# Two more chunks through seven block products, and weighted sums over 32 keys for two query blocks

## Chip, cores and metric

The kernel runs on one core of one Trainium2 chip. The metric is the device time of one execution in microseconds (us), the median of several runs. Times in the profile come from one further execution that the hardware profiler recorded. All arithmetic is fp32; matmuls run on pieces of fp32 numbers (below).

## The reference

```python
def _attn_ref(q, k, v):                       # B, H, S, D = 8, 8, 576, 64
    scores = np.matmul(q, k.transpose(0, 1, 3, 2)) / np.sqrt(D)
    rel = pos[:, None] - pos[None, :]
    mask_local = (rel >= 0) & (rel < 32)                        # heads 0 to 3
    mask_strided = (rel >= 0) & (pos[None] % 32 == pos[:, None] % 32)   # 4 to 7
    ...                                       # masked softmax over the keys
    return np.matmul(attn, v)

def _moe_ref(x, w_in, w_out):                 # x 4608x512, w_in 512x2048
    h = x @ w_in
    g = np.maximum(h, 0.0) + np.log1p(np.exp(-np.abs(h)))       # softplus
    return g @ w_out                          # w_out 2048x512

x = attn_out.transpose(0, 2, 1, 3).reshape(B * S, H * D)
return _moe_ref(x, w_in, w_out)
```

So: sparse attention, then a layer of 2048 softplus units for each of 4608 tokens, then a second layer back to 512.

## The kernel before

**Feed-forward part.** The 4608 tokens are cut into nine *chunks* of 512 (NCHUNK = 9, numbered from 0). The hidden layer of a chunk has NFC = 16 *rows* f of 128 units (HALF = 8 of them are half the layer). The 512 features are four blocks of 128. Each fp32 operand of a matmul is split into a high and a low part (x_h and x_l, gh and gl), and each block is three matmuls: high by high, high by the weights' low part, low by high. `hidden(c, f)` (line 774) makes hidden row f of chunk c in a PSUM buffer ph: four blocks by three, 12 matmuls of 128x512. Softplus of it is three steps on ScalarE (lines 786, 789, 791) and one on VectorE (line 798); ScalarE or VectorE rounds it to gh (line 290), VectorE takes the difference gl (line 828). `output(c, f)` (line 843) adds row f to the chunk's four result banks py0 to py3 (one for each 128 tokens t): 12 matmuls again. After its last row a copy on ScalarE or VectorE (`result`, line 290) brings each bank out of PSUM.

**Seven block products.** For two neighbouring chunks A and A+1, and rows f and f+HALF, the first layer is a two by two product of blocks (chunks by rows, over halves of the features). `pair_of_chunks(A, ...)` makes it in Strassen's way with seven products of six matmuls (`product`, line 946, banks a, b and c) in place of eight: 42 matmuls for 48. One such round is a *lap*; between its products stand output matmuls. Around it come evictions of banks on ScalarE (`keep`, line 1037), joining additions on VectorE (`join`, line 1042), sums of blocks of x (`x_whole`, `x_sum`, `x_sum_low`: lines 972, 978, 988; `x_sum_high` rounds on ScalarE), and sums of blocks of the weights, which are made once (`w_task`: lines 994, 1007, 1017), stored to DRAM and loaded again for each lap (`w_sum_load`, `w_near_load`, `w_away_load`). Chunks 5 and 6 go through 7 laps, 7 and 8 through 8 laps. Of chunk 6 the softplus rows are stored to DRAM and loaded again when its outputs come (`u_store`, `u_load`; it is in SPILLED); the rows of 5 and 6 that no lap makes (PLAIN: 7 and 15) are made by `hidden` beforehand.

**Attention part.** Two heads at a time make a *pair*; there are 32 pairs n, four for each batch element. Pairs 0 to 7 belong to the start, whose order is a text list, FIRST. From pair 8 on the path is: loads of q, k and v; `head_scores` (line 422, called S*n* in the plan), which multiplies 64 queries by 32 keys at a time into PSUM tiles ps and po, using a quarter of TensorE's array for each; the mask added (line 481), the softmax; `turn` on VectorE, which transposes the probabilities in three steps (a whole tile, line 550, and two halves again, lines 555 and 557); `late_sums` (line 574, V*n* in the plan), the weighted sums of v: 36 matmuls over 64 keys for 32 queries each into PSUM; and `x_part`, which casts the result to x_h (line 691, on ScalarE) and subtracts for x_l (line 689, on VectorE). x_far is a tile of x beside x_h. The sums of pair n mostly stand in one *joint* event with the scores of pair n+1, back to back on TensorE; a pair in `alone` has them by itself. Both borrow the PSUM buffers ph and the banks, so a hidden row behind them waits until `x_part` has read them out.

**What sets the order.** Each engine runs its instructions in the order in which the program issues them. From row 2 of chunk 1 on a planner sets it (class `Plan`): every piece is a task with an engine, a cost, a time at which it is due, and the tasks it comes after (S and V as above, F hidden row, O output, y result, P `turn`, L `x_part`, X and W sums of x and of weights, j joining, k eviction, Us and Ul stored and loaded rows). The list `steps` (chunk, row) is the order of hidden rows; `pair_at` says behind which of them a pair's scores stand: before, pairs 8 to 27 behind every third row, and pairs 28 to 31 inside laps 0, 2, 4 and 6 of chunks 5 and 6 (`events`). Loads and stores are issued by SyncE (SP). NEAR is the first chunk that goes through block products: `NEAR = NCHUNK - 4`.

Of the kernel before, what the change touches and what calls it, by code (L numbers as in the profile page):

```python
# [18 lines left out]
P = 128  # L19
# [97 lines left out]
def attention_softplus_ffn(  # L117
# [94 lines left out]
    turned = homes[1][:, 2 * S : 3 * S].rearrange("p (c x l) -> p c x l", c=2, l=32)  # L212
# [31 lines left out]
    ROWS[-4] = sum(both[-1:] + both[:-1], [])  # L244
    ROWS[-3] = ROWS[-4]
# [31 lines left out]
    raws = {}  # L277

# [35 lines left out]
    def load_v(n):  # L314
        b, pair = order[n]
        if n >= 2 * NPAIR:
            if n == 2 * NPAIR:
# [12 lines left out]
            return  # L330
# [71 lines left out]
    def place_of(part, h):  # L402

        return 1 - h if part == 1 else h

    def head_scores(n):
# [5 lines left out]
        for x in range(6):  # L412
            for chunk in (x, x + 3) if x > 2 else (x,):
                part = chunk // 6
                for place in range(2):
                    a, i = block_at(chunk, place) if n < 2 * NPAIR else (3 * place, chunk)
                    c = TILE * a + 32 * i
                    for h in range(2):
                        to = 64 * place + 32 * place_of(part, h)
# [126 lines left out]
    def turn(n, step):  # L546

        src = prob_of(n).rearrange("p x (c l) -> p c x l", l=32)
        if step == 0:
            nc.vector.transpose(turned, src)  # L550
            return
        for place in range(2):
            lower, upper = (slice(at, at + 32) for at in (64 * place, 64 * place + 32))
            if step == 1:
                nc.vector.transpose(turned[upper, 0], src[lower, 1])
            else:
                nc.vector.transpose(turned[lower, 1], src[upper, 0])

    def late_sums(n, joint):
# [9 lines left out]
        pos[n, 0], pos[n, 1] = to  # L569
        for x in range(NCHK):  # L570
# [290 lines left out]
    sums_r, sums_c, banks = {}, {}, {}  # L861
# [94 lines left out]
    def stage(A, i, w):  # L956

        k = {"a": 0, "b": 1, "c": 2}[w] + 3 * i
        if A < NCHUNK - 2:
            if i == 0:  # L960
                return half_of(("xw", A, k // 2), f"wi{8+k//2}", k % 2)
            if (A, w) not in sums_r:
                sums_r[A, w] = io_pool.tile([P, DM], F32, tag="io", name=f"xw_{w}_{A}")
            return sums_r[A, w]
# [25 lines left out]
    def w_whole(r, f):  # L990

        t = sums_c[r, f] = io_pool.tile([P, DM], F32, tag="io", name=f"ww_{r}_{f}")
        w = w_i(4, f + r * HALF).bitcast(F32)
# [33 lines left out]
    def w_near_load(A, f):  # L1027
        nc.sync.dma_start(w_near(A).bitcast(F32), far_w[f])

# [175 lines left out]
    for i in range(begin, len(steps)):  # L1205
# [28 lines left out]
        for t in range(nt):  # L1234
# [23 lines left out]
    def scores_of(n, x, y, name, e, cost, after, also=None):  # L1258
# [28 lines left out]
        for j, (name, step, cost) in enumerate(  # L1287
            ((f"P{n}.0", 0, 0.8), (f"P{n}.1", 1, 0.95), (f"P{n}", 2, 0.95))
        ):
            fn = lambda step=step: turn(n, step)  # L1290
            add(name, y + 8.5 + 0.9 * j, "DVE", cost, fn, after)
# [8 lines left out]
    def parts_of(n, z, made):  # L1300
# [3 lines left out]
        for c in range(NCHUNK):  # L1304
            if START[c] < first + S and START[c] + CH[c] > first:
                old = [k for k in range(c) if PLACE[k] == PLACE[c]]
                if old:
# [14 lines left out]
    for i, n in pair_at.items():  # L1322
# [5 lines left out]
        scores_of(n, x, x + 1.5, f"S{n}", "PE", cost, after, n - 1 if joint(i) else None)  # L1328
        if n == far_first:
            made, z = f"V{n}", when[i + 3] + 0.6  # L1330
            add(made, when[i + 3], "PE", 1.3, lambda n=n: sums_of(n), [f"P{n}", f"v{n}"])
        else:
            made, z = f"S{n+1}", when[i_of[n + 1]] + 1.9
        parts_of(n, z, made)
# [14 lines left out]
    def out_task(c, f, t, late=()):  # L1349
# [16 lines left out]
        e, cost, engine = (("ACT", 0.6, nc.scalar), ("DVE", 0.7, nc.vector))[t % 2 * (c > NEAR)]  # L1366
# [3 lines left out]
    u_users = [f"Us{len(steps) - 2}", f"l{len(steps) - 1}"]  # L1370
# [10 lines left out]
    def g_task(c, f, z, src, after):  # L1381
# [4 lines left out]
        e, cost, engine = ("ACT", 0.65, nc.scalar) if c in SPILLED else ("DVE", 0.45, nc.vector)  # L1386
# [20 lines left out]
    def x_task(A, z, each):  # L1407

        for i in range(2):
            x_sums(A, i, z + 10 * each * i, each)  # L1410

    def x_sums(A, i, z, each):

        n0 = NPAIR * (B - 2 if A == NEAR else B - 1)
# [3 lines left out]
        else:  # L1418
            to = {p: [f"P{p}.{A-2}.{HALF-2}"] for p in "574"}
            to["5"] += []  # L1420
        to["6"] = [f"X12.{A}.{i}"] + [f"F{NEAR+1}.{NFC-1}"] * (A == NEAR)
        room = [f"P2.{A-2}.{HALF-2}"]
        if A == NEAR:
            room = [f"F{FAR0 - NFC + 9}", "W1.0", "W1.1"]
            if i:
                room = [f"y{FAR0-1}.{t}" for t in range(TPC)]
# [3 lines left out]
        if A == NEAR and i == 1:  # L1430
            turn = "11 12 5 22 7 6 h5 l5 h6 l6 h7 l7 21 4 h4 l4".split()
# [15 lines left out]
    def w_task(f, s):  # L1447

        since = [f"F{s}", f"G{NEAR-1}.{f+HALF}"]
        if f + HALF < 10 or f + HALF > 11:  # L1450
            since = since[:1]
        for r in range(2):
            add(f"W{r}.{f}", when[s + r] + 2, "DVE", 0.75, lambda r=r: w_whole(r, f), since)
            since = [f"W0.{f}"]
        before = [f"W0.{f}", f"W1.{f}"]
        for k, p in enumerate("5763"):
            fn = lambda p=p: w_sum(p, f)
            add(f"W{p}.{f}", when[s + 2 + k // 2] + 2, "DVE", 0.42, fn, before)
# [9 lines left out]
    for k, f in enumerate((4, 5, 6, 7, 0, 1, 2, 3)):  # L1468
        w_task(f, NFC * (k // 2 + 1) + (2 if k == 7 else 3) + 6 * (k % 2) - (k == 7))

    def w_load(A, f, z):

        for r, used in ((1, "57"), (0, "63")):
            if f:
                free = [f"P{p}.{A}.{f-1}" for p in used]
            elif A == NEAR:
                free = [(f"F{FAR0 - NFC + 6}", f"F{FAR0 + 1}")[r], f"W0.{6+r}"]
            else:
                free = [f"P{p}.{A-2}.{HALF-2}" for p in used]
            fn = lambda r=r: w_sum_load(A, r, f)  # L1480
# [3 lines left out]
        elif A == NEAR:  # L1484
            free = [f"F{FAR0 - 2}"]
        else:
# [16 lines left out]
    def pair_of_chunks(A, lead, events, laps):  # L1503
# [6 lines left out]
        for f in range(laps):  # L1510
# [18 lines left out]
            s1_free = [f"u{A}.{f-1}"] if f else [f"Xl{p}.{A}.0" for p in "5674"]  # L1529
# [17 lines left out]
            gaps = (1, 0, 0, 0, 1, 2) if f == 0 and A == NEAR else (1, 0, 1, 1, 3, 2)  # L1547
# [28 lines left out]
            final = f == laps - 1  # L1576
            if final:
                soft_task(A, f + HALF, f"got.{A}.{f}")
            late = [f"P4.{A}.{f}"] if keep_u else []
            soft_task(C, f + HALF, f"j5.{A}.{f}", late, 6.0 if final else 0.0)  # L1580
            if not final:
# [3 lines left out]
            if (f, "scores") in events:  # L1585
                n = events[f, "scores"]
                also = n - 1 if n - 1 not in alone else None
                after = needs_of(n) + [f"j1.{A}.{f}", f"j2.{A}.{f}"]
                if also is not None:
                    after += [f"P{also}", f"v{also}", ring[-2]]  # L1590
                name, slots = f"S{n}", 5.5 if also is None else 10.6
                cost = slots * SLOT - Plan.WAIT
                y = now + slots * SLOT + (8 if f == laps - 1 else 0)
                scores_of(n, now, y, name, "PE", cost, [chain] + after, also)
                push(name, slots)
                events[f + 1, "free b"] = [f"Y{n}0"]
                events[f + 1, "free c"] = [f"Y{n}1"]
                if also is not None:
                    parts_of(also, now, name)
                    events[f + 1, "free c"] = [f"Y{n}1", f"L{also}0"]  # L1600
                    ring.append(f"L{also}1")
# [4 lines left out]
    on_pe(f"F{C}.{NFC-1}", 12, lambda: hidden(C, NFC - 1), [ring[-2]])  # L1606
    ring.append(f"u{C}.{NFC-1}")
    soft_task(C, NFC - 1, f"F{C}.{NFC-1}")
    w_load(NEAR, 0, when[len(steps) - 1])
    x_task(NEAR, when[len(steps) - 1] + 4, 0.1)  # L1610
    events = {(f, "scores"): far_first + 1 + k for k, f in enumerate((0, 2, 4, 6))}
    lead = [(NEAR, NFC - 1, t) for t in range(TPC)]
    laps = HALF - 1
    pair_of_chunks(NEAR, lead, events, laps)

    left = [(NEAR, g, t) for g in ROWS[NEAR][-2:] for t in range(TPC)]
    stored = {g: f"Us{g_of(C, g)}" for g in ROWS[C]}
    for at in left:
        out_task(*at)
    for k, g in enumerate(ROWS[C]):  # L1620
        z = now + 12 * SLOT * (k - 1)
        if k < 2:
            after, z = [], z - 6
        elif k < 4:
            after = [f"P1.{NEAR}.{laps-1}", f"P2.{NEAR}.{laps-1}"]
        elif k < 8:
            after = [f"u{NEAR}.{laps-1}", *stored.values()]
        else:
            after = [f"l{C}.{ROWS[C][k-4]}"]
        fn = lambda k=k, g=g: u_load(C, g, k - 2)  # L1630
        add(f"Ul{C}.{g}", z - 5, "SP", 0.8, fn, after + [stored[g]], 2.5)
        g_task(C, g, z, f"Ul{C}.{g}", [])
    for k, g in enumerate(ROWS[C][:-2]):
        if k == 7:
            name = f"V{last}"
            free = [f"j{j}.{NEAR}.{laps-1}" for j in "12"]
            after = [chain, f"P{last}", f"v{last}", *free]
            add(name, now, "PE", 1.3, lambda: sums_of(last), after)
            parts_of(last, now + 1.3, name)
            push(name, 6.4)  # L1640
        for t in range(TPC):
            out_task(C, g, t)
    A = NCHUNK - 2
# [84 lines left out]
```

## Time and profile before

| what | before |
|---|---|
| median of 3 runs | 864.33 us (864.06 to 865.29) |
| the profiled execution | 865.32 us |
| its span in the trace | 863.5 us |
| granted TensorE clock | 1.0 |
| TensorE (PE) busy | 853.9 us |
| VectorE (DVE), ScalarE (ACT) busy | 584.3 us, 494.2 us |
| GpSimd (POOL) busy | 66.4 us |

The span is what the trace covers, from the first to the last instruction; the execution's own time has 1.8 us more around it. Busy times overlap, since the engines run side by side. A row of a list of groups reads: line, engine, operation, output<-inputs, partitions x elements, how many records, then busy time and ns of one. In a timeline or in the chain a row begins with its start and length in us, and a square bracket holds the idle time ahead of it and what ended that. PSUM is the memory into which TensorE writes; a matmul record there is one instruction on the chip, and a small matmul of the attention is two of them.

### The profile page before, as it was taken

What the parts mean: (1) busy time and instruction counts of PE and PEld (TensorE: products, weight loads), DVE (VectorE), ACT (ScalarE), POOL (GpSimd) and SP (SyncE); (2) the same over time, 40 slices, a digit from 0 to 9 for tenths busy, and PEclk for the clock granted to TensorE, in tenths of its full rate; (3) what the DMA queues carried; (4) which work ended last, traced back from release to release, by engine and by line L of the source; (5) the groups of instructions that cost most, each with busy time, mean ns of one, the idle gap of its engine ahead of it and who ended that gap; (6) DMA issues with size and microseconds to landing.
All of it is one profiled execution on the core that took longest, in us unless ns stands there. A gap on an engine that the chain in (4) does not pass through costs nothing.

```text
span 863.5 us, 18656 instructions
## 1 busy us (share of the span) xinstructions
PE 853.9 (99%) x7688; PEld 703.3 (81%) x7688; DVE 584.3 (68%) x1106; ACT 494.2 (57%) x913; POOL 66.4 (8%) x89
## 2 busy tenths in 40 slices
PE   7999999999999999999999999999999999999998
PEld 5787888888888888888888888788888888888886
DVE  7899977677686668776668866666687645656500
ACT  6998755665555555646555655766664355566400
POOL 6345550000000000000000000000000000000000
PEclk9999999999999999999999999999999999999999
DMA  9894215556422554326424543655546144333100
GB/s 325 286 354 152 58 47 195 184 161 217 137 84 90 171 149 130 104 80 200 130 76 149 155 125 118 198 177 187 174 148 209 50 158 135 109 123 122 45 29 24
DMA packets 85332, 124.49 MB, mean 144 GB/s; under 512 B 7296, under 2 KB 52480, under 8 KB 85248
## 3 DMA queue, kind: packets, MB, share of 16 engines
q1 hardware_dynamic: 84960, 122.99, 43.8%
q8 instruction: 60, 0.98, 0.5%
q10 hardware_dynamic: 288, 0.33, 0.1%
q14 instruction: 24, 0.20, 0.1%
HBM read 92.88 MB, written 30.41 MB: 143 GB/s over the span
## 4 chain that ended last, share of the span: by engine, by line
PE 93%; DMA 2%; DVE 2%; ACT 1%; issue 1%; POOL 0%; SPq 0%; ACTq 0%; POOLq 0%
PE py L843 43%; PE ph L774 24%; PE bank_a L946 10%; PE bank_c L946 5%; PE po L574 2%; PE bank_b L946 2%; DMA ro<-in_moe_w_out_dram 2%; PE ps L422 2%; PE py_last L843 1%; PE po L422 1%; PE pv L574 1%; PE pv L640 1%; PE pt L610 1%; DVE home L536 1%; DMA raw_q<-in_qk_dram 0%
## 5 line engine op out<-in xcount | busy, mean ns | idle before, releaser
L843 PE MATMUL py<-w_o,gh 128*128 128x512 f32 x1024 | 318.3, 392 | 0.0
L843 PEld LDWEIGHTS py<-w_o,gh 128*128 128x128 f32 x1024 | 190.4, 188 | 39.5
L774 PE MATMUL ph<-x_h,w_i 128*128 128x512 f32 x656 | 202.7, 390 | 0.5 <-DVE u L798 0.5
L843 PE MATMUL py<-w_o,gl 128*128 128x512 f32 x512 | 199.2, 389 | 0.0
L774 PEld LDWEIGHTS ph<-x_h,w_i 128*128 128x128 f32 x656 | 122.5, 188 | 26.7 <-POOL home L525 0.9
L774 PE MATMUL ph<-x_l,w_i 128*128 128x512 f32 x328 | 127.6, 389 | 0.0
L843 PEld LDWEIGHTS py<-w_o,gl 128*128 128x128 f32 x512 | 96.1, 188 | 20.2
L290 ACT CAST gh<-u 128x512 fp32r<-128x512 f32 x89 | 55.1, 621 | 96.4 <-DVE u L798 74.5
L786 ACT ACTIVATE u<-ph 128x512 f32<-128x512 f32 x84 | 50.2, 599 | 94.8 <-PE ph L774 92.2
L828 DVE TENSOR_TENSOR gl<-u,gh 128x512 fp32r<-128x512 f32 x117 | 80.8, 691 | 25.0 <-ACT gh L290 21.9
L789 ACT ACTIVATE u<-u 128x512 f32<-128x512 f32 x144 | 90.9, 633 | 3.8
L791 ACT ACTIVATE u<-u 128x512 f32<-128x512 f32 x144 | 90.8, 631 | 3.7
L798 DVE SCALAR_TENSOR_TENSOR u<-ph,u 128x512 f32<-128x512 f32 x84 | 57.7, 687 | 37.3 <-ACT u L791 36.6
L774 PEld LDWEIGHTS ph<-x_l,w_i 128*128 128x128 f32 x328 | 61.6, 188 | 13.0
L786 ACT ACTIVATE u<-kept 128x512 f32<-128x512 f32 x45 | 28.5, 633 | 42.4 <-DVE kept L1042 26.0
L290 DVE COPY o<-py 128x512 f32<-128x512 f32 (+1 forms) x15 | 10.0, 670 | 47.0 <-PE py L843 46.8
L481 DVE TENSOR_TENSOR home<-ps,home 128x384 f32<-128x384 f32 x28 | 15.5, 555 | 36.4 <-PE ps L422 34.9
L1042 DVE TENSOR_TENSOR kept<-bank_c,kept 128x512 f32<-128x512 f32 x15 | 10.4, 692 | 36.5 <-PE bank_c L946 35.2
L290 ACT COPY home<-home 128x576 f32<-128x576 f32 x26 | 33.5, 1290 | 1.6 <-DMA home<-in_qk_dram 1.6
L290 ACT COPY o<-py 128x512 f32<-128x512 f32 (+1 forms) x21 | 11.5, 575 | 38.1 <-PE py L843 27.3
L1037 ACT COPY kept<-bank_a 128x512 f32<-128x512 f32 x30 | 17.7, 589 | 25.5 <-PE bank_a L946 24.5
L422 PEld LDWEIGHTS ps<-home,home 64*32 64x32 f32 x1344 | 23.3, 106 | 9.9 <-issue 8.1
(205 smaller groups left out, 1299.5 us busy)
## 6 DMA issues: line engine op xcount, KB each, us to landing
home<-in_qk_dram SPq DMA_DIRECT2D x56, 288.0 KB, 3.5
ws<-far SPq DMA_DIRECT2D x30, 512.0 KB, 3.3
out_dram<-o SPq DMA_DIRECT2D x35, 256.0 KB, 2.3
ri<-in_moe_w_in_dram SPq DMA_DIRECT2D x16, 512.0 KB, 7.3
ro<-in_moe_w_out_dram SPq DMA_DIRECT2D x16, 512.0 KB, 8.3
far_w<-w_i SPq DMA_DIRECT2D x16, 512.0 KB, 4.5
w_i<-far_w SPq DMA_DIRECT2D x16, 512.0 KB, 3.4
near<-far_w SPq DMA_DIRECT2D x15, 512.0 KB, 3.3
```

What stands on the lines that cost most here:

```text
L290: (engine.copy if engine is nc.scalar else engine.tensor_copy)(dst, src)
L422: nc.tensor.matmul(pss[n, part][to : to + 32, at : at + 64], lhsT=qT[head, c : c + 32], rhs=k_of(n)[head, c : c + 64], start=True, stop=True,)
L574: nc.tensor.matmul(to[place][64 * h : 64 * h + 64, 32 * x : 32 * x + 32], lhsT=v_late[rows, x, D * h : D * h + D], rhs=turned[rows, place_ ...
L774: nc.tensor.matmul(ph, lhsT=w_i(c, f)[:, half, cc * P : (cc + 1) * P], rhs=x_at(x, cc, c), start=(i == 0), stop=(i == 3 * NCC - 1),)
L786: nc.scalar.activation(us[c, f], phs[c, f], AF.Abs)
L789: nc.scalar.activation(u, u, AF.Exp, scale=-1.0)
L791: nc.scalar.activation(u, u, AF.Ln, bias=1.0)
L798: nc.vector.scalar_tensor_tensor(to, in0=ph, scalar=0.0, in1=u, op0=ALU.max, op1=ALU.add)
L828: engine.tensor_tensor(g, us.pop((c, f)), ghs[c, f].bitcast(F32), op=ALU.subtract)
L843: nc.tensor.matmul(y_of(c, t), lhsT=g[:, sl], rhs=w32["o", f][:, half], start=(f == ROWS[c][0] and n == 0), stop=(f == ROWS[c][-1] and n = ...
L946: nc.tensor.matmul(bank, lhsT=w_left(p, A, f, half, i), rhs=x_right(p, A, part, i), start=p in "125" and n == 0, stop=n == 5, skip_group_c ...
L1037: nc.scalar.copy(kept(A, s), bank_of(p, A, f))
```

## The change

**Chunks 3 and 4.** NEAR becomes 3: chunks 3 and 4 go through seven laps as 5 and 6 did, chunk 4's rows being stored and loaded as well (SPILLED is now 4 and 6). The sums of weights are made earlier, during chunks 1 and 2, and each chunk pair makes its own 12 sums of x. Rows 7 and 15 of the new pairs are plain hidden rows again: 3.7, 3.15 and 4.7 at the end of `steps`, 4.15 before the first lap; rows 6.7, 6.15, 5.7 and 5.15 between outputs of chunk 4.

**Weighted sums.** For pairs 8 to 31 `turn` is one transpose of 32x32 blocks. `late_sums` works by 32 keys and two neighbouring query blocks (64 queries): 38 matmuls, the last two of them with 32 queries. A PSUM bank now collects from two row groups of the array, with `start` for the first key block and `stop` for the last. v is loaded as four quarters of 32 partitions.

**Places of the pairs.** Pairs 8 to 20 stand behind steps 0, 2, 5, 8, ... 30 counted from row 2 of chunk 1, so two or three rows apart; pairs 21 to 25 in laps 1 to 5 of chunks 3 and 4; the sums of 24, pairs 26 and 27 between outputs of chunk 4; 28 to 31 as before.

The core of the diff:

```diff
-    SPILLED = (NCHUNK - 3,)
-    PLAIN = [(NCHUNK - 3, HALF - 1), (NCHUNK - 3, NFC - 1)]
+    WHOLE = range(2 * NPAIR, 8 * NPAIR)
+    NEAR = 3
+    SPILLED = (NEAR + 1, NEAR + 3)
+    PLAIN = [(c, f) for c in SPILLED for f in (HALF - 1, NFC - 1)]
...
     def load_v(n):
+        if is_whole(n):
+            src = v[b, pair].rearrange("(x l) (h d) -> l x h d", l=32, h=2)
+            for quarter in range(4):
+                place, h = divmod(quarter, 2)
+                lo = 1 - place
+                rows = slice(32 * quarter, 32 * quarter + 32)
+                keys = src[:, NCHK * place + lo - 1 : NCHK * place + NCHK, h]
+                nc.sync.dma_start(v_whole[rows, lo:], keys)
+            return
...
     def turn(n, step):
+        if is_whole(n):
+            blocks = prob_of(n).rearrange("p x (c l) -> p (x c) l", l=32)
+            nc.vector.transpose(turned_all.rearrange("p (x l) -> p x l", l=32), blocks)
+            return
...
+        if is_whole(n):                       # in late_sums
+            for x in range(NCHK + 1):
+                for quarter in range(4):
+                    place, h = divmod(quarter, 2)
+                    if x + place == 0:
+                        continue
+                    lo, hi = max(64 * x - 32, 0), min(64 * x + 32, 64 * NCHK)
+                    at = max(32 * x - 32, 0)
+                    rows = slice(32 * quarter, 32 * quarter + 32)
+                    nc.tensor.matmul(
+                        to[place][64 * h : 64 * h + 64, at : at + hi - lo],
+                        lhsT=v_whole[rows, x],
+                        rhs=turned_all[rows, lo:hi],
+                        start=x + place == 1,
+                        stop=x == NCHK,
...
-    NEAR = NCHUNK - 4
-    steps += [(NEAR, HALF - 1), (NEAR + 1, HALF - 1), (NEAR, NFC - 1)]
+    steps += [(NEAR, HALF - 1), (NEAR, NFC - 1), (NEAR + 1, HALF - 1)]
-    far_first = last - NPAIR
-    pair_at = {begin + 3 * i: n for i, n in enumerate(range(2 * NPAIR, far_first + 1))}
+    far_first = 5 * NPAIR
+    places = (0, 2, 5, 8, 11, 14, 16, 18, 20, 23, 25, 27, 30)
+    pair_at = {begin + i: n for i, n in zip(places, range(2 * NPAIR, far_first + 1))}
-    alone = (far_first, last)
+    alone = (last - NPAIR - 3, last - NPAIR, last)
...
-    events = {(f, "scores"): far_first + 1 + k for k, f in enumerate((0, 2, 4, 6))}
+    events = {(f, "scores"): far_first + 1 + k for k, f in enumerate((1, 2, 3, 4, 5))}
+    pair_of_chunks(NEAR, [(NEAR, NFC - 1, t) for t in range(TPC)], events, HALF - 1)
+    n = last - NPAIR
+    A = NEAR + 2
+    between = [                               # between chunk 4's outputs
+        (2, 10.6, lambda: pair_of_heads(n - 1, done)),
+        (6, 10.6, lambda: pair_of_heads(n, done)),
+        (10, 6.4, lambda: sums_alone(n, [f"L{n-1}{half}" for half in range(2)])),
+        (11, 12, lambda: plain(A + 1, HALF - 1)),
+        (13, 12, lambda: plain(A + 1, NFC - 1)),
+        (14, 12, lambda: plain(A, HALF - 1)),
+        (15, 12, lambda: plain(A, NFC - 1)),
+    ]
+    spilled(NEAR, ROWS[C], between, finish)
...
+    events = {(f, "scores"): n + 1 + k for k, f in enumerate((0, 2, 4, 6))}
+    pair_of_chunks(A, [(A, NFC - 1, t) for t in range(TPC)], events, HALF - 1)
```

Three places of the order show the moves that the prediction speaks of. A name ends in chunk and row (ph_3_15: hidden row 3.15) or in the pair (pv_19), then a buffer number; x16 means sixteen such instructions in a row.

First TensorE, where the plain hidden rows of the first block-product pair begin. Before, in front of chunk 5, pair 27's sums are followed by the outputs of row 4.12, and then by hidden row 4.15:

```order
L774 MATMUL ph_4_14_6137<-x_l3_594,w_i_4_14_6088 128x512
L574 MATMUL pv_27_0_6159<-home_1_95,home_0_94 64x32 x2
L574 MATMUL pv_27_1_6160<-home_1_95,home_0_94 64x32 x2
...
L843 MATMUL py0_106<-w_o_12_1644,gh_4_12_6125 128x512 x2
...
L843 MATMUL py3_109<-w_o_12_1644,gl_4_12_6134 128x512
L774 MATMUL ph_4_15_6228<-x_h0_364,w_i_4_15_6127 128x512 x2
```

Now, in front of chunk 3, the scores of pair 20 and the sums of pair 19 (in tiles po_20 and pv_19) come behind hidden row 3.7:

```order
L813 MATMUL ph_3_7_4220<-x_l3_594,w_i_7_1034 128x512
L439 MATMUL ps_20_4241<-home_2_96,home_0_94 32x64 x16
L439 MATMUL po_20_4242<-home_2_96,home_0_94 32x64 x4
...
L600 MATMUL pv_19_1_4279<-home_1_95,home_0_94 64x32 x2
L600 MATMUL po_20_4242<-home_1_95,home_0_94 64x64 x2
L600 MATMUL pv_19_1_4279<-home_1_95,home_0_94 64x64 x2
...
L600 MATMUL pv_19_1_4279<-home_1_95,home_0_94 64x32 x2
L813 MATMUL ph_3_15_4338<-x_h0_364,w_i_2_15_4107 128x512 x2
```

The sums changed their shape (64x32 to 64x64), and a hidden row stands straight behind them where an output row stood.

Second ScalarE at the same entry. Before, the roundings of the sums of x stood elsewhere, and the results of the chunk that ends (o_4) came behind two rows' softplus:

```order
L786 ACTIVATE u_5_7_6296<-ph_5_7_6267 128x512
L789 ACTIVATE u_5_7_6296<-u_5_7_6296 128x512
L791 ACTIVATE u_5_7_6296<-u_5_7_6296 128x512
L290 CAST gh_5_7_6314<-u_5_7_6296 128x512
...
L290 COPY o_4_0_6336<-py0_106 128x512
L290 COPY o_4_2_6343<-py2_108 128x512
```

Now roundings of sums of x (line 1022) and of two rows stand ahead of chunk 2's first result, o_2_0:

```order
L730 CAST x_h3_592<-pv_19_1_4279 128x8x16
L730 CAST x_far_3_4326<-pv_19_1_4279 128x10x16
L825 ACTIVATE u_3_7_4330<-ph_3_7_4220 128x512
...
L825 ACTIVATE u_3_15_4364<-ph_3_15_4338 128x512
...
L1022 CAST t_7_3_1_4385<-xw_3_0_3925 128x512
L298 CAST gh_3_7_4405<-u_3_7_4330 128x512
L1022 CAST t_4_3_1_4423<-xw_3_0_3925 128x512
L298 CAST gh_3_15_4428<-u_3_15_4364 128x512
L298 COPY o_2_0_4431<-py0_106 128x512
```

Between the last softplus and the copy five ScalarE instructions now wait for VectorE's operations. Third, VectorE's transposes of one pair, before:

```order
L550 STREAM_TRANSPOSE home_1_95<-home_1_95 128x576
L555 STREAM_TRANSPOSE home_1_95<-home_1_95 32x288 x2
L557 STREAM_TRANSPOSE home_1_95<-home_1_95 32x288 x2
```

and now, one instruction for five:

```order
L567 STREAM_TRANSPOSE home_1_95<-home_1_95 128x576
```

On each engine the program holds, before and after: hidden-row matmuls 1008 and 672, block-product matmuls 630 and 924, output matmuls 1728 in both, matmuls of sums (line 574 or 600) 864 and 912; VectorE joinings 45 and 66, sums of x (three lines) 48 and 72; ScalarE evictions 45 and 66; transfers issued by SyncE 382 and 456.

More of the change, by code (lines that the diff above doesn't have):

```diff
@@ L1385, in g_task @@
             after = after + [g_room(c, f)]
-        e, cost, engine = ("ACT", 0.65, nc.scalar) if c in SPILLED else ("DVE", 0.45, nc.vector)
+        e, cost, engine = ("DVE", 0.45, nc.vector) if c > NEAR + 3 else ("ACT", 0.65, nc.scalar)
         add(f"h{n}", z, e, cost, lambda: g_high(c, f, engine), [src] + after)
@@ L1485, in w_load @@
             free = [f"F{FAR0 - 2}"]
+        elif A == NEAR + 2:
+            free = [f"F{c}.{HALF-1}" for c in (A, A + 1)]
         else:
@@ L1492, in w_load @@
             free = [f"F{NEAR+1}.{NFC-1}"]
+        elif A == NEAR + 2:
+            free = [f"F{c}.{NFC-1}" for c in (A, A + 1)]
         else:
@@ L1586, in pair_of_chunks @@
                 n = events[f, "scores"]
[L1587 to L1594, printed above, removed]
@@ L1595, in pair_of_chunks @@
-                push(name, slots)
+                pair_of_heads(n, [f"j1.{A}.{f}", f"j2.{A}.{f}"], 8 if f == laps - 1 and A > NEAR else 0)
                 events[f + 1, "free b"] = [f"Y{n}0"]
                 events[f + 1, "free c"] = [f"Y{n}1"]
[L1598 to L1601, printed above, removed]
+                if n - 1 not in alone:
+                    events[f + 1, "free c"] = [f"Y{n}1", f"L{n-1}0"]
@@ new lines, in pair_of_heads @@
+    def pair_of_heads(n, free, wait=0.0):
+        also = n - 1 if n - 1 not in alone else None
+        after = needs_of(n) + free
+        if also is not None:
+            after += [f"P{also}", f"v{also}", f"L{n-2}0", ring[-2]]
+        name, slots = f"S{n}", 5.5 if also is None else 10.6
+        cost = slots * SLOT - Plan.WAIT
+        y = now + slots * SLOT + wait - 1
+        scores_of(n, now, y, name, "PE", cost, [chain] + after, also)
+        push(name, slots)
+        if also is not None:
+            parts_of(also, now, name)
+            ring.append(f"L{also}1")
@@ new lines, in sums_alone, with plain, spilled @@
+    def sums_alone(n, free):
+        name = f"V{n}"
+        after = [chain, f"P{n}", f"v{n}", f"Y{n}0", f"Y{n}1", *free]
+        add(name, now, "PE", 1.3, lambda: sums_of(n), after)
+        parts_of(n, now + 1.3, name)
+        push(name, 6.4)
+    def plain(c, f):
+        on_pe(f"F{c}.{f}", 12, lambda: hidden(c, f), [ring[-2], *lows_of(c), *row_loads.get(f, [])])
+        ring.append(f"u{c}.{f}")
+        soft_task(c, f, f"F{c}.{f}")
+    def spilled(A, rows, between, finish=None):
+        C, end = A + 1, HALF - 2
+        for g in ROWS[A][-2:]:
+            for t in range(TPC):
+                out_task(A, g, t)
+        if finish:
+            finish()
+        stored = {g: f"Us{g_of(C, g)}" for g in ROWS[C]}
+        start = now
+        for k, g in enumerate(ROWS[C]):
+            z = start + 12 * SLOT * (k - 1)
+            z += sum(slots * SLOT for at, slots, _ in between if at < k)
+            if k < 2:
+                after, z = [], z - 6
+            elif k < 4:
+                after = [f"P1.{A}.{end}", f"P2.{A}.{end}"]
+            elif k < 8:
+                after = [f"u{A}.{end}", *stored.values()]
+            else:
+                after = [f"l{C}.{ROWS[C][k-4]}"]
+            fn = lambda k=k, g=g: u_load(C, g, k - 2)
+            add(f"Ul{C}.{g}", z - 5, "SP", 0.8, fn, after + [stored[g]], 2.5)
+            g_task(C, g, z, f"Ul{C}.{g}", [])
+        for k, g in enumerate(rows):
+            for at, _, fn in between:
+                if at == k:
+                    fn()
+            for t in range(TPC):
+                out_task(C, g, t)
@@ L1616, in attention_softplus_ffn @@
[L1616 to L1643, printed above, removed]
+    x_task(NEAR, when[len(steps) - 6], 0.5, 20)
+    events = {(f, "scores"): far_first + 1 + k for k, f in enumerate((1, 2, 3, 4, 5))}
```

150 lines of the change are left out of this document (89 added, 61 removed).

## The prediction

> **What bounds the kernel now.** I read the page's busy shares and its chain first, then TensorE's list of waits, then the chain in order of time around the places that the change touches, and last the timelines of the engines that feed TensorE.
>
> ```profile
> span 863.5 us, 18656 instructions
> ...
> PE 853.9 (99%) x7688; PEld 703.3 (81%) x7688; DVE 584.3 (68%) x1106; ACT 494.2 (57%) x913; POOL 66.4 (8%) x89
> ...
> PE 93%; DMA 2%; DVE 2%; ACT 1%; issue 1%; POOL 0%; SPq 0%; ACTq 0%; POOLq 0%
> ```
>
> The chain that ended last runs through TensorE for 93% of the span; the rest lies in the start. So a matmul taken away shortens the run by its pace, unless the engine then waits. TensorE's own waits, longest first (us, times, longest):
>
> ```profile
> PE pt L610 <- issue: 2.8, 2, 1.6
> ...
> PE ph L774 <- DVE u L798: 0.5, 1, 0.5
> ```
>
> They belong to the first stage, which this change leaves alone. After it the engine runs without a break, as the chain around the first block products shows (start, us, what):
>
> ```profile
> 504.05 2.72 PE ph L774 x12
> 506.77 1.18 PE pv L574 x72
> 507.95 2.95 PE py L843 x12
> ...
> 521.77 2.72 PE ph L774 x12
> 524.49 2.72 PE py L843 x12
> ...
> 542.85 1.37 PE bank_a L946 x6
> 544.25 0.70 DVE kept L1042
> 544.95 0.04 issue
> 545.00 1.66 PE bank_a L946 x6
> 546.65 1.36 PE py L843 x6
> ...
> 549.00 1.59 PE bank_a L946 x6
> ...
> 610.11 1.36 PE py L843 x6
> ...
> 613.64 1.58 PE bank_a L946 x6
> ```
>
> Twelve matmuls of 512 columns take 2.72 us in a hidden row, in an output row, and (six in 1.36) in a product: 0.2267 us each. There is one wait: block product 4 of the first lap starts at 545.00, where its six take 1.66 instead of 1.36; about 0.27 us is lost to the joining addition.
>
> **The products.** For chunks 3 and 4, seven laps of seven products of six matmuls take the place of 7 x 48 matmuls: 294 for 336, so 42 fewer. All lie on the path: 42 x 0.2267 = 9.52 us less. The 1728 output matmuls stay.
>
> **The weighted sums.** 36 matmuls over 64 keys and 32 queries become 38 over 32 keys and 64 queries (the last two have 32). On the chip each is two records:
>
> ```profile
> 506.70 1.25 PE L574 MATMUL pv<-home,home 64*64 64x32 f32 x72
> ...
> 611.40 0.48 PE L422 MATMUL ps<-home,home 64*32 64x64 f32 x20
> ...
> L574 PE MATMUL pv<-home,home 64*64 64x32 f32 x936 | 29.7, 220 | 0.0
> ...
> L422 PE MATMUL ps<-home,home 64*32 64x64 f32 x1344 | 27.8, 220 | 0.0
> ```
>
> Seventy-two records in 1.25 us, the last of 0.22: 71 steps of 14.5 ns, 58 ns for four. The scores, with 64 columns over half the weights, take 19 steps in 0.26 us, 55 ns for four. The new form has the columns of the one and the weight width of the other, still four tiles of the array at once. If weights and columns pass beside each other, as both rows suggest (neither shows the sum of the two), four records cost the larger, 58 ns: 19 groups for 18, 0.058 us more for a pair of heads. The other end is that they pass one after the other or two tiles at a time, 116 ns: 19 x 116 - 18 x 58 = 1.16 us more. Below nothing it can't go by these rows: no group of four took less than 55, and 19 x 55 is still no less than 18 x 58. I take 58, the row with the same weights: 24 pairs x 0.058 = 1.4 us more.
>
> [...] The scores' first twenty records go to one PSUM tile, ps, from two groups of rows (head 0 and head 1), and run at 55 ns for four. [...]
>
> **One more split.** Pair 24's sums and pair 25's scores now stand apart. Together they take, in the chain, 613.64 - 611.47 = 2.17, plus 0.22 in the longer next product; apart, scores 549.00 - 548.01 = 0.99 plus 0.23, sums 1.18 plus 0.23: 2.63. That is 0.24 us more; I take 0.2. The other splits are moved, not added.
>
> **VectorE, ScalarE, the queues.** Removed are 96 half transposes; added are 24 operations that make sums of x, 21 joinings, and on ScalarE 21 evictions and 8 roundings:
>
> ```profile
> L555 DVE STREAM_TRANSPOSE home<-home 32x288 f32<-32x288 f32 x38 | 17.9, 470 | 0.9
> L557 DVE STREAM_TRANSPOSE home<-home 32x288 f32<-32x288 f32 x38 | 17.8, 470 | 0.5
> ...
> L972 DVE TENSOR_TENSOR xw<-x_h,x_l 128x512 f32<-128x512 f32 x2 | 1.4, 682 | 0.0
> ...
> L1037 ACT COPY kept<-bank_a 128x512 f32<-128x512 f32 x30 | 17.7, 589 | 25.5 <-PE bank_a L946 24.5
> ```
>
> VectorE: 45 x 0.68 - 96 x 0.47 = -14 us; ScalarE: 29 x 0.59 = +17 us and the rounding of chunk 3's softplus, which moves from VectorE. Neither total is on the path: they hide beside TensorE while each has a free third. The transfers (14 more of weight sums, 16 more softplus rows out and 16 in, 24 more of v in quarters, 12 fewer streamed weights) run under it too; the nearest, a v load, lands in 4.2 us where pairs stand at least 13 us apart, so I cost them at nothing. If that cover goes, the sums of a pair wait.
>
> ```profile
> home<-in_v_dram SPq DMA_DIRECT2D x24, 256.0 KB, 4.2
> ```
>
> **Where covers do go: the entry to chunk 3.** The new order puts hidden row 3.15 straight behind pair 19's sums; until now twelve outputs always stood there. Pair 18 of before shows what they hid. First TensorE, then ScalarE, then VectorE:
>
> ```profile
> 321.73 0.73 PE L843 MATMUL py<-w_o,gh 128*128 128x512 f32 x2
> ...
> 324.58 0.62 PE L774 MATMUL ph<-x_h,w_i 128*128 128x512 f32 x2
> ```
> ```profile
> 319.67 0.60 ACT L786 ACTIVATE u<-ph 128x512 f32<-128x512 f32 x1 [2.13 <-PE ph L774]
> 320.30 0.63 ACT L789 ACTIVATE u<-u 128x512 f32<-128x512 f32 x1
> ...
> 321.84 0.27 ACT L691 CAST x_h<-po 128x128 fp32r<-128x128 f32 x1 [0.25 <-PE pv L574]
> ...
> 322.53 1.30 ACT L290 COPY home<-home 128x576 f32<-128x576 f32 x1
> ```
> ```profile
> 323.89 0.31 DVE L689 TENSOR_TENSOR x_far<-pv,x_far 128x160 fp32r<-128x160 f32 x1
> 324.13 0.68 DVE L798 SCALAR_TENSOR_TENSOR u<-ph,u 128x512 f32<-128x512 f32 x1
> ```
> ```profile
> 231.63 0.68 DVE L290 COPY o<-py 128x512 f32<-128x512 f32 x1
> 232.23 0.68 DVE L828 TENSOR_TENSOR gl<-u,gh 128x512 fp32r<-128x512 f32 x1
> ```
>
> Row 3.15 takes over the PSUM buffer of those sums, so it waits for two casts and two subtractions: the casts start 0.1 us after the sums (321.84 against 321.73) and take 0.5 for two, the last subtraction 0.31, with hand-overs about 1.0 us. If VectorE is late by a Strassen operation it is 1.6, if early 0.8. The softplus of row 3.7 comes behind the casts on ScalarE: three steps of 0.63, then 0.68 on VectorE, ending 3.2 us after the sums.
>
> Then chunk 3's first output needs chunk 2's first result out of its bank, and the new ScalarE order sets that copy behind the rounding of x sum 4, which VectorE makes late. Counted from the end of the sums, with VectorE at 0.60 an operation (232.23 - 231.63): row 3.7 ends 3.2; four x operations and subtractions 5.5; row 3.15's softplus (ScalarE first does its copy of 1.30) 6.8; six more operations 10.7; ScalarE's roundings and the copy, 3 x 0.6, 12.5. TensorE comes there at 1.0 + 4 x 2.72 = 11.9: 0.7 us of wait (0 to 2.5). A third, 0.3: an x operation stands ahead of the subtraction on which row 2.14 waits, and pair 18 above had 324.58 - 324.20 = 0.38 to spare. And 0.2 for the results behind it. Entry: 2.2 us, between 0 and 5.
>
> The first lap's wait of 0.27 now comes twice: +0.27.
>
> **The sum.** -9.52 + 1.4 + 0.2 + 2.2 + 0.27 = -5.45 us. The profiled execution took 865.32 us (span 863.5) and would take 859.9; the median of the runs is 864.33, 1.0 below it, so I predict 859.0.
>
> **Rivals.**
> - *The covers hold.* VectorE has lost its half transposes and may come to the entry early; the waits there shrink to 0.5: 857.2. For it: before, no regular place waited. Against: the order at row 3.15 leaves nothing between. Chance 0.2.
> - *VectorE becomes the bound where pairs stand 13.1 us apart* (two rows of 5.44 and a pair of 2.3). Between the mask additions of pairs 17 and 18 stand some 15 large operations and 8 small: 15 x 0.68 + 8 x 0.3 = 12.6 us. Its fullest stretch so far without a wait was 16.4 of 20:
>
> ```profile
> 480.00:500.00 20.00, 20.00 (x223) 16.56 (x222) 16.39 (x32) 11.63 (x20) 0.00 (x0) 1.00 0.62 190
> ```
>
>   Against: overlapped at 0.60 they are 11.4. If each of the five closest intervals costs 0.8: 863.0. Chance 0.16.
> [...]
> - *Nothing comes of it*, the 42 matmuls being given back in waits at both entries: 864. Chance 0.03.
>
> **How the numbers follow.** The likeliest case, 0.53, is 859.0, on its own 857.6 to 861.3. From 856.5 to 863.2 lies all but the half-pace case, the last rival and the outer parts of the covers and of VectorE as bound, about 2 in 10. About 0.2% (1.7 us) is what a measurement can tell from no change. Faster by more than that (below 862.6): 0.53, 0.2 and nearly two thirds of 0.16, 0.83; slower (above 866.1): 0.08; the same: 0.09.
>
> **What would show it.** Right: 672 matmuls in the hidden line and 924 in the products; 76 records of sums at 58 ns for four; TensorE waiting at hidden row 3.15 for a subtraction, and at chunk 3's first output for a result's copy; no wait inside the laps. Wrong: sums taking over 1.4 us, a wait at each pair's sums for the transpose or for v, or VectorE over 90% busy where the pairs stand close.

## The result, and the profile after

| | before | changed |
|---|---|---|
| median | 865.01 us (864.06 to 865.98, 6 runs) | 870.63 us (869.40 to 875.21, 6 runs) |
| ratio | | 1.0073 (95% interval 1.005 to 1.0096) |

The change made the kernel slower by 0.7%; 859.0 was predicted. The page of the changed kernel, and its TensorE waits (us, times, longest):

```profile
span 873.4 us, 18955 instructions
...
PE 856.8 (98%) x7742; PEld 703.4 (81%) x7742; DVE 557.0 (64%) x1039; ACT 515.5 (59%) x958; POOL 65.8 (8%) x88
...
PE 91%; DVE 4%; ACT 2%; issue 2%; DMA 1%; POOL 0%; SPq 0%; ACTq 0%; DVEq 0%; POOLq 0%
```
```profile
PE pt L649 <- issue: 4.5, 2, 3.8
PE py L882 <- DVE o L298: 2.0, 2, 1.2
PE py L882 <- ACT o L298: 1.5, 2, 0.8
PE ph L813 <- DVE x_far L728: 1.3, 1, 1.3
```

TensorE is busier than before (856.8 for 853.9 us) although 42 large matmuls are gone, and it waits at three places where it did not. The first line belongs to the start: this profiled execution (875.21) lost some 4 us there, with a granted clock of 0.83 between 20 and 40 us, which the median does not contain. So I count from the first wait behind the start, which both profiles have (hidden row, 75.6 before and 80.2 after): 784.0 us before, 789.2 after, to TensorE's last matmul: 5.2 more. The medians lie 5.6 apart.

**Scores and sums.** Two events that stand alone show the price without any wait: pair 8's scores, and a pair's sums with what follows. Timeline of TensorE (start, us, what), before and then after:

```profile
133.60 0.48 PE L422 MATMUL ps<-home,home 64*32 64x64 f32 x20
...
134.59 0.73 PE L843 MATMUL py<-w_o,gh 128*128 128x512 f32 x2
...
507.88 0.73 PE L843 MATMUL py<-w_o,gh 128*128 128x512 f32 x2
```
```profile
138.21 0.65 PE L439 MATMUL ps<-home,home 64*32 64x64 f32 x32
...
139.35 0.72 PE L882 MATMUL py<-w_o,gh 128*128 128x512 f32 x2
...
475.89 1.35 PE L600 MATMUL pv<-home,home 32*64 32x32 f32 x76
477.18 0.73 PE L882 MATMUL py<-w_o,gh 128*128 128x512 f32 x2
```

From the first record to the next large matmul the scores take 1.14 us instead of 0.99, the sums 1.29 instead of 1.18 (from 506.70). Both together are 0.25 us for a pair before rounding, 6.0 for 24. The scores were not meant to change, but one line of the diff, which the prediction passed over, does change them:

```diff
-    def place_of(part, h):
-        return 1 - h if part == 1 else h
+    def place_of(part, h, n=0):
+        return 1 - h if part == 1 and not is_whole(n) else h
```

`place_of` names the 32 partitions into which a head's scores go. For the last three of the nine query blocks (part 1) the two heads used to exchange their places; the new sums need them unexchanged. Each score matmul multiplies 32 queries by 64 keys on an eighth of the array (64*32 in the rows above, where a large matmul has 128*128), and not 64 by 32 on a quarter, as the description of the kernel before has it. Counted by the 64 rows that it reads and the 32 partitions that it writes, a pair uses eight such parts with the exchange and four without it.

**The entry to chunk 3.** The chain of the changed kernel in order of time, and the copy at 346.15 in ScalarE's timeline:

```profile
333.82 0.32 DVE x_far L728
...
334.28 5.72 PE ph L813 x24
340.00 6.13 PE py L882 x27
...
346.15 0.59 ACT o L298
...
348.49 0.70 DVE o L298
...
351.62 0.70 DVE o L298
```
```profile
346.15 0.58 ACT L298 COPY o<-py 128x512 f32<-128x512 f32 x1 [0.28 <-PE py L882]
```

Hidden row 3.15 waits for pair 19's subtraction, until 334.28. Then 27 output matmuls run, rows 2.13 and 2.14 and three of row 2.15, and TensorE waits for a copy which had waited for TensorE itself: the order holds chunk 3's first py0 straight behind chunk 2's last py0. The same comes back for other banks.

**The entry to chunk 5.** Timeline of all engines:

```profile
537.88 0.42 SPq L852 DMA_DIRECT2D u_in<-far_u  x1
538.39 5.07 SPq L898 DMA_DIRECT2D out_dram<-o  x3
540.36 0.58 ACT L298 COPY o<-py 128x512 f32<-128x512 f32 x1 [2.38 <-DMA out_dram<-o]
541.00 0.73 PE L882 MATMUL py<-w_o,gh 128*128 128x512 f32 x2 [0.78 <-ACT o L298]
542.41 0.69 DVE L298 COPY o<-py 128x512 f32<-128x512 f32 x1 [4.18 <-DMA out_dram<-o]
543.16 0.73 PE L882 MATMUL py<-w_o,gh 128*128 128x512 f32 x2 [1.19 <-DVE o L298]
```

The third and fourth copy of chunk 4's results wait for the stores of the first and second. The pool of tiles for results has four buffers, and the reloads of rows 6.7 and 6.15 (u_in) hold two of them until chunk 6's outputs.

### The profile page after: what moved, and what is told of

Its sections match the earlier page's. It is cut to its first block, busy times and chain, and to the rows that moved or that the text cites. A ratio compares the mean times of both kernels' runs of the same rounds, so it can differ in the third digit from the quotient of the medians.

```text
span 873.4 us, 18955 instructions
## 1 busy us (share of the span) xinstructions
PE 856.8 (98%) x7742; PEld 703.4 (81%) x7742; DVE 557.0 (64%) x1039; ACT 515.5 (59%) x958; POOL 65.8 (8%) x88
## 4 chain that ended last, share of the span: by engine, by line
PE 91%; DVE 4%; ACT 2%; issue 2%; DMA 1%; POOL 0%; SPq 0%; ACTq 0%; DVEq 0%; POOLq 0%
PE py L882 42%; PE ph L813 14%; PE bank_a L985 14%; PE bank_c L985 7%; PE bank_b L985 3%; PE pv L600 3%; PE ps L439 2%; PE py_last L882 1%; PE po L439 1%; PE pv L679 1%; PE pt L649 1%; PE po L600 1%; DVE home L553 1%; DVE a_i L767 0%; DMA raw_q<-in_qk_dram 0%
## 5 line engine op out<-in xcount | busy, mean ns | idle before, releaser
L813 PE MATMUL ph<-x_h,w_i 128*128 128x512 f32 x416 | 129.4, 392 | 1.8 <-DVE x_far L728 1.3
L813 PEld LDWEIGHTS ph<-x_h,w_i 128*128 128x128 f32 x416 | 77.3, 188 | 19.6 <-issue 1.3
L813 PE MATMUL ph<-x_l,w_i 128*128 128x512 f32 x208 | 81.0, 389 | 0.0
L825 ACT ACTIVATE u<-ph 128x512 f32<-128x512 f32 x56 | 33.3, 597 | 57.5 <-PE ph L813 54.9
L825 ACT ACTIVATE u<-kept 128x512 f32<-128x512 f32 x66 | 41.7, 631 | 39.8 <-DVE kept L1085 29.9
L837 DVE SCALAR_TENSOR_TENSOR u<-ph,u 128x512 f32<-128x512 f32 x56 | 38.3, 683 | 26.5 <-ACT u L830 26.4
L813 PEld LDWEIGHTS ph<-x_l,w_i 128*128 128x128 f32 x208 | 39.1, 188 | 8.4
L1080 ACT COPY kept<-bank_a 128x512 f32<-128x512 f32 x44 | 25.8, 587 | 26.4 <-PE bank_a L985 26.4
L1085 DVE TENSOR_TENSOR kept<-bank_b,kept 128x512 f32<-128x512 f32 x22 | 15.2, 692 | 36.9 <-PE bank_b L985 36.9
L985 PE MATMUL bank_a<-t,away 128*128 128x512 f32 x132 | 33.8, 391 | 0.2
```

What stands on the lines that cost most here:

```text
L813: nc.tensor.matmul(ph, lhsT=w_i(c, f)[:, half, cc * P : (cc + 1) * P], rhs=x_at(x, cc, c), start=(i == 0), stop=(i == 3 * NCC - 1),)
L825: nc.scalar.activation(us[c, f], phs[c, f], AF.Abs)
L837: nc.vector.scalar_tensor_tensor(to, in0=ph, scalar=0.0, in1=u, op0=ALU.max, op1=ALU.add)
L985: nc.tensor.matmul(bank, lhsT=w_left(p, A, f, half, i), rhs=x_right(p, A, part, i), start=p in "125" and n == 0, stop=n == 5, skip_group_c ...
L1085: nc.vector.tensor_tensor(t, bank_of(p, A, f), t, op=ALU.add)
```

## The experiments

All kernels shared the runs of the kernel before, whose median was 864.4 to 864.7 in them. Where an expectation speaks of an event's price, it counts from the start of the large matmul ahead, less 0.2267, which is 0.09 more than between the rows above.

**e1: products without the new sums.**

```diff
-    WHOLE = range(2 * NPAIR, 8 * NPAIR)
+    WHOLE = range(0)
```

> The changed kernel with scores, transposes, loads of v and sums as before, everything else as changed. Theory: the new form costs 0.252 us in every joint event (2.514 against 2.262), 0.149 of it in the scores, which is 6.05 us over 24 pairs; so 870.6 - 6.05 = 864.6, with the joint event back at 2.262, and up to 1 us more where VectorE's half transposes come back at the entries. Rival, the prediction's price (58 ns for four, 1.4 us in all): 869.2.

869.58 us (865.92 to 872.32; ratio 1.0054, 1.0038 to 1.0069): neither was right for the time. The joint events are back at 2.262, and 6 us of TensorE's work are gone, but waits took their place: at the sums of pairs 8 and 18 (0.8 and 0.9), at hidden rows 2.14 and 3.15 (0.9 and 2.4), and at the entry to chunk 5 (3.3). Another 1.0 in its profile is a slower clock behind the wait at row 3.15 (last section). So the new form does buy something; e7 looks at what.

**e2: the new sums without the products.** The functions of the new form put into the kernel before.

> The kernel before with only the new sums (38 matmuls over 32 keys, one transpose, four loads of v, scores without the exchange of heads); products and places of the pairs as before. Theory: joint event 2.514, 865.0 + 6.05 = 871.1, and no wait of TensorE that was not there. Rival, the prediction's price: 866.4. Rival, that the events are longer because the pairs stand closer: 865.0 and 2.262, since the places are the old ones.

871.16 us (870.39 to 872.04; ratio 1.0072, 1.0057 to 1.0087): the first theory, to 0.1 us. TensorE's timeline has the same two events, with no wait anywhere:

```profile
132.23 0.65 PE L438 MATMUL ps<-home,home 64*32 64x64 f32 x32
...
133.37 0.72 PE L881 MATMUL py<-w_o,gh 128*128 128x512 f32 x2
...
510.43 1.35 PE L599 MATMUL pv<-home,home 32*64 32x32 f32 x76
511.71 0.74 PE L881 MATMUL py<-w_o,gh 128*128 128x512 f32 x2
```

1.14 and 1.28. The price belongs to the form, not to closer pairs.

**e3: the exchange of heads brought back, in the scores alone.**

```diff
-        return 1 - h if part == 1 and not is_whole(n) else h
+        return 1 - h if part == 1 else h
```

> The changed kernel with the scores' exchange of the two heads in the last three of nine query blocks as before (the sums then take the other head's probabilities there; nothing else differs in what is issued). Theory: the exchange lets neighbouring groups of four use the other four tiles of the array; scores alone 1.081 instead of 1.230, the joint event 2.365, 24 x 0.149 = 3.6 us less: 867.0. Rival, the scores are slowed by the sums behind them or by closer pairs: joint event stays 2.51 and the time 870.6.

The sums here leave the exchange out. The joint event is 2.364, as expected, and the scores alone take 0.99 again. The time is 868.65 us (ratio 1.0046, 1.003 to 1.0061), a gain of 2.0 and not 3.6. In its profile the entry to chunk 5 took part of that back: the same two waits as above, and behind them a slower clock (last section).

**e4: two reloads later.** Only the place of two transfers changes.

```diff
-                after, z = [], z - 6
+                after, z = [f"y{A-1}.{t}" for t in range(TPC) if A > NEAR], z - 6
```

> The changed kernel with the reload of rows 6.7 and 6.15 put behind chunk 4's four results. Theory: these reloads hold two of the four buffers that the results use, so the third and fourth copy wait for a store of 3 to 4 us; with them later the waits of 0.94 and 1.36 at the entry to chunk 5 go: 868.3. Rival, the copies are late because ScalarE and VectorE are: the waits stay within 0.3 us, 870.6.

868.08 us (ratio 1.004, 1.0026 to 1.0055), and both waits are gone; the buffers were the cause. SyncE's timeline, results first and then the reloads:

```profile
534.19 2.48 SPq L898 DMA_DIRECT2D out_dram<-o  x4
536.77 1.14 SPq L852 DMA_DIRECT2D u_in<-far_u  x2
```

Its profile shows another wait, which was 0.2 in the changed kernel and is 1.4 here. First TensorE's list of waits, then the chain:

```profile
PE pv L600 <- DMA home<-in_v_dram: 1.1, 2, 0.6
```
```profile
476.88 3.98 DMA home<-in_v_dram
...
480.90 0.24 PE pv L600
```

Pair 24's sums, alone at 471, and pair 25's, at 478, stand 7 us apart, and v of pair 25 can only come when 24's is used up.

**e5: the order mended at four places.** The edit of e4, and:

```diff
+        if i == FAR0 + 1:                 # row 3.15 behind row 2.13's outputs
+            after.append(f"O{FAR0-3}")
...
+            if c == NEAR:                 # chunk 3's outputs behind row 2.15's
+                own.append(f"O{FAR0-1}")
...
-        (2, 10.6, lambda: pair_of_heads(n - 1, done)),
-        (6, 10.6, lambda: pair_of_heads(n, done)),
-        (10, 6.4, lambda: sums_alone(n, [f"L{n-1}{half}" for half in range(2)])),
-        (11, 12, lambda: plain(A + 1, HALF - 1)),
+        (3, 10.6, lambda: pair_of_heads(n - 1, done)),
+        (7, 10.6, lambda: pair_of_heads(n, done)),
+        (11, 6.4, lambda: sums_alone(n, [f"L{n-1}{half}" for half in range(2)])),
+        (12, 12, lambda: plain(A + 1, HALF - 1)),
```

> The changed kernel with four changes of order: the reloads of rows 6.7 and 6.15 behind chunk 4's results; chunk 3's first output behind all four outputs of row 2.15; row 2.13's outputs between pair 19's sums and hidden row 3.15; pairs 25 to 27 one output row later, so that pair 25's v has time behind pair 24's sums. Theory: each wait has its own cause in the order; 1.3 us at row 3.15, 2.0 at chunk 3's first outputs, 2.3 at the entry to chunk 5 and 0.2 to 1.4 at pair 25's sums go, new ones stay under 0.5: 870.6 - 5.4 = 865.2. Rival, the prediction's reading (ScalarE and VectorE are too late at chunk 3's entry for any order): 0.7 to 2 us of wait stay there, 867.

863.14 us (862.24 to 864.68; ratio 0.9984, 0.9976 to 0.9993), 2 us better than expected. None of the four places has a wait now; of the four edits only the reloads were also tried alone (e4). The chain at the entry to chunk 3 runs on TensorE without a break:

```profile
328.02 2.95 PE py L882 x12
330.97 5.44 PE ph L813 x24
336.41 8.16 PE py L882 x36
344.57 2.72 PE ph L813 x12
```

So ScalarE and VectorE are not too late there for every order; the wait came from the order.

**e6: the new form only where pairs stand close**, in the order of e5.

```diff
-    WHOLE = range(2 * NPAIR, 8 * NPAIR)
+    WHOLE = (8, *range(14, 21), 25, 26, 27)
```

> The order of e5, and the old scores, transposes, loads of v and sums for the thirteen pairs that stand three rows or a lap apart (9 to 13, 21 to 24, 28 to 31), the new ones for the eleven that stand closer. Theory: 13 x 0.252 = 3.3 us less than e5, since VectorE has time for the half transposes there: 861.9. Rival, the half transposes come late everywhere once the products' additions are there: waits of 0.5 to 1 us at each of those pairs, 865 or more.

859.38 us (859.11 to 859.98; ratio 0.9941, 0.9927 to 0.9954). This version beats both kernels, and no sums wait in it: 3.8 us less than e5, of which 13 x 0.25 is 3.3 and the rest a wait of 0.6 at one pair's sums in e5's profile. Its page:

```profile
span 857.6 us, 18881 instructions
...
PE 847.6 (99%) x7690; PEld 698.0 (81%) x7690; DVE 582.7 (68%) x1091; ACT 514.3 (60%) x958; POOL 66.4 (8%) x91
```

**e7: the old form everywhere**, in the order of e5 (`WHOLE = range(0)`).

> The order of e5 with the old form for all pairs. Theory: 24 x 0.252 = 6.05 us less than e5 on TensorE, but where pairs stand two rows apart VectorE's half transposes end late and TensorE waits, 0.8 to 1 us at some four of the eleven places: 865.2 - 6.05 + 3.5 = 862.7. Rival, those waits of e1 came from the entries' bad order: 859.2.

863.89 us (861.83 to 866.97; ratio 0.9992, 0.998 to 1.0004): worse than expected, but on the theory's side; 4.5 us slower than e6 with less work on TensorE. Timelines of VectorE and TensorE at pair 18's sums:

```profile
305.47 0.97 DVE L576 STREAM_TRANSPOSE home<-home 32x288 f32<-32x288 f32 x2
306.46 0.97 DVE L578 STREAM_TRANSPOSE home<-home 32x288 f32<-32x288 f32 x2
307.46 0.69 DVE L837 SCALAR_TENSOR_TENSOR u<-ph,u 128x512 f32<-128x512 f32 x1
```
```profile
308.20 0.25 PE L613 MATMUL pv<-home,home 64*64 64x32 f32 x2 [0.75 <-DVE u L837]
```

The half transposes of the pair push a hidden row's softplus back by 2 us, and the sums need the PSUM buffer which that softplus reads. Such waits stand at the sums of pairs 8 (0.8) and 18 (1.0), at the block product behind pair 20's sums (1.1), and at hidden rows 2.14 and 3.15 behind pairs 18 and 19 (0.9 and 2.4). At least one place does not have e5's order: here the planner put row 2.13's outputs ahead of pair 19's sums, so that row 3.15 stands straight behind them again, while in e5 and e6 twelve outputs (2.95 us) stand between.

**e8: the exchange kept, the turns taken away**, in the kernel before.

```diff
-        for x in range(6):
-            for chunk in (x, x + 3) if x > 2 else (x,):
+        for x in range(9):
+            for chunk in (x,):
```

> The kernel before with its scores' nine query blocks in plain order, 0 to 8, the exchange of heads kept; only the order of 36 matmuls differs. Theory: what made the scores fast is that blocks with and without the exchange take turns, so that a group of four finds its four tiles free; in plain order 1.081 becomes 1.23, and 24 x 0.14 = 3.4 us more: 868.0. Rival, the exchange itself matters (which rows write which partitions), not the turns: 1.081 and 864.65.

865.98 us (864.92 to 869.38; ratio 1.002, 1.001 to 1.003). Neither: the scores alone take 1.04 us, nearer to 0.99 than to 1.14.

```profile
132.80 0.71 PE L422 MATMUL ps<-home,home 64*32 64x64 f32 x36
133.30 0.24 PE L422 MATMUL po<-home,home 64*32 64x64 f32 x1
133.33 0.24 PE L422 MATMUL ps<-home,home 64*32 64x64 f32 x4
...
133.84 0.74 PE L843 MATMUL py<-w_o,gh 128*128 128x512 f32 x2
```

With the exchange the turns are worth 0.05 (0.99 against 1.04). The other 0.10 up to e2's 1.14 (turns, no exchange) is what the exchange is worth without them, if turns alone save nothing, which no run shows. The rows show what differs: the program issues all 48 records of ps first, yet the first po record starts behind 36 of them. Exchanged blocks read the same 64 rows as the others and write the 32 partitions that those leave free, and the weight loads (PEld) for them come ahead too, behind 40 of 48:

```profile
132.80 0.60 PEld L422 LDWEIGHTS ps<-home,home 64*32 64x32 f32 x40 [0.35 <-issue]
133.30 0.13 PEld L422 LDWEIGHTS po<-home,home 64*32 64x32 f32 x2
```

In e2, without the exchange, the records start in the order of the program, 32 of ps first. The small matmuls of e8, then, do not start in the order of the program, which the description of the kernel before has every engine keep; nor do those of the kernel before, whose first po record starts behind 20 of ps where the program has 32. Why no more po records come ahead in e8 is not shown.

The exchange together with the new sums was not tried: the sums of one head would then come into the same partitions of a PSUM bank from two row groups, and no run here shows whether that gives the right sums.

**e9: the new form for four pairs**, in the order of e5 (`WHOLE = (8, 18, 19, 20)`).

> The order of e5, and the new form only for the four pairs whose sums waited in e7 (8, 18, 19, 20); the old form for the other twenty. Theory: the new form is worth its 0.252 us only where VectorE's half transposes end too late, which e7 showed at these four places; seven more old pairs than e6 take 7 x 0.252 = 1.8 us off, 857.6, with no wait at any sums. Rival, taking load off VectorE at pairs 14 to 17 is what kept pairs 18 to 20 in time in e6: waits of about 1 us come back at two or three of them and a wait at hidden row 2.14 with them, 860 to 861.

861.01 us (860.16 to 862.98; ratio 0.9958, 0.9945 to 0.9972): the rival. Pair 17's sums wait 0.9 now, and hidden row 3.15 again; the engine's list of waits:

```profile
PE bank_a L985 <- issue: 1.8, 2, 1.0
PE ph L813 <- DVE x_far L728: 1.3, 1, 1.3
```

VectorE's lateness moves from pair to pair. The second wait also stands because, with these tasks, the planner put row 2.13's outputs ahead of the event and not behind it, as in e7. What the first line is, two breaks inside a product in chunks 3 and 4, the profile doesn't show; the profiled execution, 862.98, is the slowest of the five.

## Why the prediction was wrong

By its own terms (us; measured in the profile of the changed kernel against that of before):

| term | predicted | measured |
|---|---|---|
| products, 42 x 0.2267 | -9.5 | -9.5 |
| weighted sums | +1.4 | +2.5, and +3.6 in the scores |
| one more split | +0.2 | +0.2 |
| entry to chunk 3 | +2.2 | +4.0 |
| entry to chunk 5 | 0 | +2.5 |
| lap 0 twice | +0.27 | +0.4 |
| three other short waits | 0 | +1.1 |
| sum | -5.45 | +4.8, of 5.2 in all |

A wait stands in the right column with the 0.1 us by which the matmul behind it starts late. The 0.4 us left lies in steps a few ns longer than the usual 227: their mean is 227.0 ns before and 227.2 after.

- **Products**: right; the median step between large matmuls is 227 ns in both kernels, and the mechanism holds in e5 and e6.
- **Weighted sums**: the step that failed first. It took the sums' 58 ns for four, and they have them; slower steps in the first and last groups, which are not full, make it 0.10 for a pair instead of 0.058. (Six matmuls have 32 queries, the first two and the last four, and not two.) But it priced only the 38 matmuls and not what the new form asks of its neighbour: the scores lost their exchange, 0.15 for a pair, shown by e2, e3 and e8. This alone is 3.6 us, and it stood in the diff. The signs by which the prediction would have known itself right came, 58 ns for four among them, but none of them looked at the scores.
- **The half-pace case**, 0.08 of the forecast, fell: no run shows its 116 ns for four. Each bank of the new sums is written from two row tiles, and the 76 records take 1.29 us, at 58 ns for four. The two tiles write different halves of its partitions.
- **Entry to chunk 3**: the wait at row 3.15 was right in place and cause, 1.3 for 1.0; that at row 2.14 was 0.2 for 0.3. The wait at chunk 3's first output came at the place that was named, but not from ScalarE's queue; the order of TensorE's own rows makes it, three times over (0.8, 0.3, 0.9). e5 shows it.
- **Transfers cost nothing**: wrong twice. The step asked whether a transfer lands in time, and not which buffer it holds meanwhile: the reloads at the entry to chunk 5 took two of the four (e4). And "pairs stand at least 13 us apart" was wrong for pairs 24 and 25 (7 us).
- **VectorE as the bound**: not with the new form, which kept it in time in all but small waits; but with the old form at the new places it is (e1, e7). That is what the new form is worth: e6 has it at the eleven pairs that stand close, where it costs 11 x 0.25 = 2.8 us, and is still 4.5 faster than e7 (3.4 in the profiled executions), so it saves some 6 to 7 us there. Of these up to 2.4 belong to row 3.15, where e7's order differs too; an old form with e6's order at that place was not run. At the other thirteen pairs the new form costs 3.3 and buys nothing. The stretch that the prediction took for VectorE's fullest without a wait of TensorE, 16.4 us of 20, was not that: from 100 to 120 us it was busy for 19.3.
- **The lap's wait** comes twice, as predicted.

## What to carry to other kernels

When a part changes the layout of its input, price the part that makes this layout too: here an unchanged count of matmuls became 15% slower because its results had to lie elsewhere. For every transfer that is moved, ask not only when it lands but which buffer it holds until it is used, and who else takes from that pool. And a form that relieves an engine is worth its price only where that engine is late: use it there.

## What the runs showed of the hardware

Behind some waits of TensorE stood a slower clock, which cost time again. In e3's profile two waits (0.75 and 1.31 us) stand close together at the entry to chunk 5, and the next matmuls start 0.43 us apart for 3 us instead of 0.23. TensorE's timeline, and the granted clock (third number from the end) in three stretches:

```profile
536.15 1.22 PE L882 MATMUL py<-w_o,gh 128*128 128x512 f32 x2 [1.31 <-DVE o L298]
537.17 0.63 PE L882 MATMUL py<-w_o,gl 128*128 128x512 f32 x1
537.60 2.37 PE L985 MATMUL bank_a<-x_far,near 128*128 128x512 f32 x6
```
```profile
533.00:536.60 3.60, 1.54 (x5) 0.94 (x5) 1.20 (x2) 1.12 (x2) 0.00 (x0) 0.91 0.48 179
536.60:539.60 3.00, 3.00 (x9) 2.27 (x9) 0.79 (x2) 0.62 (x1) 0.00 (x0) 0.54 0.24 90
539.60:543.00 3.40, 3.40 (x16) 2.80 (x15) 0.69 (x1) 1.22 (x2) 0.00 (x0) 1.00 0.19 34
```

The clock falls to 0.54 behind 3.6 us in which TensorE was busy for 1.54. In e1's profile it falls to 0.56, from 332.3 to 335.0 us, behind the wait of 2.4 us at row 3.15; there TensorE was busy for 3.02 of the 5.3 us before. The profile of the changed kernel has the same two waits as e3's (0.78 and 1.19), and e7's the same wait at row 3.15 (2.3), and neither has such a fall: the clock is 1.00 from 540.6 to 549 us in the first and 1.0 over the whole span in the second. So it came in two of these four profiles. It is likely why kernels with such waits spread wider (e7 over 5.1 us, e6 without them over 0.9): the two fastest executions of e7 (861.83 and 862.81) were granted a clock of 1.0 over the whole span, the two slowest (866.38 and 866.97) 0.996. It is likely, too, why e5 gained more than its waits, by 2 us. No run tested that link by itself. The longest idle stretch ahead of the fall was 1.3 us in e3 and 2.3 in e1, while e7's of 2.3 had no fall behind it; what brings the fall is not shown.
